# A wait on GpSimd for the VectorE instruction planned ahead of it, and output stores issued by two engines

## The chip, the cores and the metric

The program runs on one core of one Trainium2 chip. The core has five engines that each work through their own instruction list in order: TensorE (PE in the profile; PEld is its weight load), VectorE (DVE), ScalarE (ACT), GpSimd (POOL) and SyncE (SP, which here only issues DMAs). They meet through semaphores. The metric is the device time of one execution in microseconds. Before the change it is 690.68 us, the median of three runs (690.0 to 691.18). The profile was taken from one further execution of 688.92 us.

## What is computed

Three stages follow each other, all in float32 with tight precision:

```python
# 1. attention with random features, per batch and head (4 x 8 x 576 x 64, 128 features)
phi(x) = exp(h - max(h)) / sqrt(m),   h = x @ omega.T - |x|^2 / 2
num = phi(q) @ (phi(k).T @ v);  den = phi(q) @ sum_s phi(k) + 1e-6
x = num / den                            # then reshaped to 2304 tokens x 512
# 2. gated projection
x = (sigmoid(x @ w_gate) * (x @ w_val)) @ w_out        # 512 -> 1536 -> 512
# 3. soft mixture: 8 experts with 4 slots each
logits = x @ phi
slots  = softmax(logits, over tokens).T @ x             # 32 slots x 512
out    = softmax(logits, over slots) @ (max(slots @ w1[e], 0) @ w2[e])
```

## The kernel before

**Tiling.** The 2304 tokens are cut into five column blocks, four of 512 and one of 256. For stage 2 the hidden width 1536 is cut into 12 chunks of 128. A step is one block with one chunk: 12 products of 128x512 for the gate (tile `ga`), 12 for the value (tile `va`) and 12 for the way down (tiles `o0` to `o3`). There are 12 and not 4 because a float32 product is made of three passes: both operands are split into a high part in a shorter format and a low part that holds the rest, and high x high, high x low and low x high are added (function `three`). The first block is done in two pieces, with the second block between them.

**Who makes the operands.** `split_w` makes the two parts of each weight: the high part is a copy on ACT or DVE, the low part a subtraction (`w<-ws,w`, in the first steps `w<-x,w`), which POOL may do and mostly does. The three weights of a step have one tile each (`w0`, `w1`, `w2`), so POOL's subtraction for the next step has to lie between PE's last use of the tile and the first low pass that needs it. POOL also squares the attention's inputs (`g<-g`) and makes the low parts of the attention's results (`XT<-g,XT`). In the first third of the run the weights arrive as 64-bit words and are turned into float32 by a chain of integer instructions on ACT and DVE (`convert`, tile `x2T`, result in `x`), are written to DRAM (`wscr`), and are read back for the later blocks (`ws`). The attention's work is spread over the same third; its results leave PSUM through DVE and ACT (`g`, `g1b`).

**Who sets the order.** Nothing is issued as the code meets it. Every call is recorded in a `Plan` (class `Plan`, L104); `schedule` (L236) then runs a list scheduler over all of them with a cost per instruction (`cost`, L200) and writes one order for each engine, and `issue` (L398) hands the instructions out in that order. `cost` returns two values: a duration and whether the instruction holds the port that DVE and POOL share. By this table every POOL instruction holds it, and those of DVE that neither touch PSUM nor reduce. While one of the two holds it, the planner starts no port-holding instruction on the other (`port` in `schedule`). This is a rule of the plan alone. In the built program DVE and POOL wait for each other only where one reads or overwrites what the other wrote; when DVE runs later than planned, POOL starts its instruction as soon as its own inputs are there, whether or not DVE has done what was planned ahead of it.

**The end.** `combine` (L1106) makes the output in two column halves of 384 and 128 columns. PE's products go to PSUM, DVE and ACT copy them to SBUF, and `store` (L1118) issues 16 DMAs to the output, all from SP: six of 384 KB, two of 384 KB and two of 192 KB for the first half, four of 256 KB and two of 64 KB for the second.

All instructions but a few stand under one line of the profile, L405, since `issue` hands them out there; they are told apart by engine and tile.

Of the kernel before, what the change touches and what calls it, by code (L numbers as in the profile page):

```python
# [20 lines left out]
B, H, S, D, M = 4, 8, 576, 64, 128  # L21
# [7 lines left out]
HEAD, TAIL = 512, S - 512  # L29
# [74 lines left out]
class Plan:  # L104
# [95 lines left out]
    def cost(self, eng, method, kw, outs, ins):  # L200


        if method == "together":
            return TURN * (eng == "PE" and kw["parts"][0][2][0].ap[0][1] < 128) + sum(self.cost(eng, a[1], a[3], o, i)[0] for a, o, i in kw["parts"]), False
        o = outs[0] if outs else None
        n = self.free(o) if o is not None else 0
        if eng == "PE":
            if method == "transpose":
                return 0.109 * max(0.5, o.ap[0][1] / 128), False
            if ins[0].dtype == F32R:  # L210
                return (n + 32) / 2400.0, False
            if o.ap[0][1] == 32:
                return max(0.43 * n / 256, 0.055) / 4, False
            if o.ap[0][1] == 64:
                return max(n / 600.0, 0.21) / 2 + 0.12, False
            return max(0.222, n / 600.0) * (ins[0].ap[0][1] / 128 if o.ap[0][1] == 128 else 1.0), False
        ni = max([n] + [self.free(a) for a in ins])
        psum = any(a.space == bass.MemoryType.PSUM for a in ins + outs)
        if eng == "ACT":
            return (0.07 if psum else 0.11) + 0.00083 * ni + 0.09 * sum(self.free(a) == 1 for a in ins), False  # L220
        if eng == "DVE":
            if method == "reciprocal":
                return 0.06 + 0.0054 * n, False
            if method == "tensor_tensor_reduce":
                return 0.075 + ni / 960.0, False
            if method == "tensor_reduce" or psum:
                return 0.067 + ni / 960.0, False
            if method in ("tensor_tensor", "scalar_tensor_tensor"):
                return 0.067 + ni / 960.0, True
            return 0.067 + ni / 1920.0, method != "memset"  # L230
        if eng == "POOL":
            return 0.1 + 0.00225 * ni, True
        return 0.06, False
# [165 lines left out]
        assert len(order) == n, (len(order), n)  # L399
        return order  # L400

    def issue(self):
        for _, _, (e, method, a, k) in self.schedule():
            for e, method, a, k in [p[0] for p in k["parts"]] if method == "together" else [(e, method, a, k)]:
                getattr(self.eng[e], method)(*a, **k)  # L405


def body(ctx, tc, nc, qkT, tok, von, omT, wall, phi, w1, w2, ident_d, srep_d, rrep_d, mask_d, out):
    plan = Plan(nc)
    PE, ACT, DVE, POOL, SP = (Eng(plan, e) for e in ("PE", "ACT", "DVE", "POOL", "SP"))  # L410
# [6 lines left out]
    def T(shape, tag, dtype=F32, bufs=1):  # L417
        return plan.tile(sb, shape, dtype, tag, bufs)
# [12 lines left out]
    def copy(dst, src, eng=("ACT", "DVE")):  # L431
        hi_of(dst, src, eng)
# [76 lines left out]
    def turn(lst, name):  # L509
        ring[name] = ring.get(name, -1) + 1  # L510
        return lst[ring[name] % len(lst)]
# [4 lines left out]
    def bank(tag=None):  # L516
        if tag is None:
            tag = turn(FLW, "fl") if wide[0] else "fl"
        tag = "fl" if tag in POOLED else tag
        return plan.tile(psp, [128, 512], F32, tag, NFL if tag == "fl" else 1, dyn=tag == "fl")  # L520
# [585 lines left out]
    def combine(half, po):  # L1106

        (c0, w), t0 = COLS[half], plan.t
        Pf, P = (T([128, 512], "ga_a", F32, 2)[:, 0:w] for _ in range(2))
        DVE.tensor_copy(out=Pf, in_=po)  # L1110
        ps = bank("o2")[:, 0:w]
        PE.matmul(ps, rrep, Pf, start=True, stop=True)
        DVE.tensor_copy(out=P, in_=ps)
        tags = (["fl", "ga", "va", "o3", "fl", "o0"], ["fl", "ga", "va", "o3", "fl", "o0", "o1", "o2"])[half]
        rows = out.rearrange("(b s) d -> s b d", s=S)
        cols = slice(c0, c0 + w)

        def store(ob, j, z, n):  # L1118
            if j == NB - 1:
                for y in range(2):  # L1120
                    SP.dma_start(out=rows[HEAD:S, y::2, cols], in_=ob[TAIL * y:TAIL * y + TAIL])
                return
            r = S * j + 128 * z
            SP.dma_start(out=out[r:r + 128 * n, cols].rearrange("(z p) d -> p z d", p=128), in_=ob)

        def product(ps, j, z):
            r = slice(32 * z, 32 * z + 32)
            PE.matmul(ps, cT[r, j, :], P[r], start=True, stop=True)

        if half == 0:  # L1130
            tiles = [(j, z) for j in range(NB) for z in range(BLOCKS[j][1] // 128)]
            for a in range(0, len(tiles), 6):
                part6 = tiles[a:a + 6]
                plan.t = t0 + 30.0 * (a == 12)
                pb = [bank(turn(tags, "out0"))[:, 0:w] for _ in part6]
                plan.together(lambda: [product(ps, j, z) for ps, (j, z) in zip(pb, part6)])
                for k in range(0, 6, 2):
                    ob = free.pop(0)[:, 0:2 * w].rearrange("p (z d) -> p z d", z=2)
                    for y in range(2):
                        copy(ob[:, y, :], pb[k + y], (("DVE", "ACT"), ("ACT", "DVE"))[y])  # L1140
                    store(ob, *part6[k], 2)
            plan.t = t0
            return
        for js in ((0, 1), (2, 3), (4,)):
            n = BLOCKS[js[0]][1] // 128
            ob = free.pop(0).rearrange("p (j z d) -> p j z d", j=2, z=4)[:, 0:len(js), 0:n]
            pb = [bank(turn(tags, "out1"))[:, 0:w * len(js)].rearrange("p (j d) -> p j d", d=w) for _ in range(n)]
            plan.together(lambda: [product(pb[z][:, k], j, z) for k, j in enumerate(js) for z in range(n)])
            for z in range(n):
                copy(ob[:, :, z], pb[z], (("DVE", "ACT"), ("ACT", "DVE"))[z % 2])  # L1150
            for k, j in enumerate(js):
                store(ob[:, k], j, 0, n)
# [6 lines left out]
    for h in range(2):  # L1159
        r = slice(64 * h, 64 * h + 64)  # L1160
# [99 lines left out]
    i = 0  # L1260
# [50 lines left out]
        plan.t += 2.0  # L1311
        combine(half, po)
    with tc.manual_schedule():
        plan.issue()


def layout(q, k, v, omega, moe_w_gate, moe_w_val, moe_w_out, moe2_phi, moe2_w1, moe2_w2):
# [42 lines left out]
def build(nc, arrays):  # L1360
    args = [nc.dram_tensor(n, a.shape, mybir.dt.from_np(a.dtype), kind="ExternalInput").ap()
            for n, a in arrays.items()]
    args.append(nc.dram_tensor("out_0", (NTOK, DM), F32, kind="ExternalOutput").ap())
    with tile.TileContext(nc, schedule_with_timeline_sim=True) as tc:
        with ExitStack() as ctx:
            body(ctx, tc, nc, *args)
# [8 lines left out]
```

## Time and profile before

| what | value |
|---|---|
| median of three runs | 690.68 us (690.0 to 691.18) |
| the profiled execution | 688.92 us, span of its instructions 687.1 us |
| PE busy | 663.6 us, 97% |
| DVE, ACT, POOL busy | 457.7, 429.0, 288.7 us |
| TensorE's granted clock | full up to the last slice |

The span is what lies between the first and the last instruction of the profile; 1.8 us of the execution lie around it. A busy share is an average over stages that differ: PE's 97% holds a long middle in which PE hardly pauses, a start and an end where it waits for DMAs, and a few short pauses between 60 and 215 us. Idle time of another engine costs nothing unless PE waits for it there.

### The profile page before, as it was taken

The page shows a single profiled execution, that of the slowest core. Times are in us where ns is not written, and L with a number is a line of the kernel's source. Part 1 is how long each engine was busy: PE and PEld are TensorE (multiplying, and loading weights), DVE is VectorE, ACT ScalarE, POOL GpSimd, SP SyncE. Part 2 cuts the span into 40 slices and gives each one's busy share as a digit, 9 for nine tenths or more (in the row PEclk, how much of TensorE's full clock was granted, in tenths as well). Part 3 has the DMA queues.
Part 4 walks back from the last instruction along what each step waited for, and adds up shares of the span by engine and source line. Part 5 has one row for each costly group of instructions (what it writes and reads, how often), then busy time and mean ns, then how long its engine had stood idle before and what let it go on. Part 6 is the DMA issues. An engine that isn't in the chain of part 4 may idle for free.

```text
span 687.1 us, 12505 instructions
## 1 busy us (share of the span) xinstructions
PE 663.6 (97%) x4366; PEld 533.8 (78%) x4366; DVE 457.7 (67%) x1299; ACT 429.0 (62%) x962; POOL 288.7 (42%) x245
## 2 busy tenths in 40 slices
PE   7999899999999999999999999999999999999994
PEld 5676577778787888788788888788888789999672
DVE  3899999899997575666666555567444335666413
ACT  5899788888787574766566675554344445675002
POOL 0566445565334343434444543434444444553100
PEclk9999999999999999999999999999999999999997
DMA  8889766777965336443444222589622328666978
GB/s 288 314 271 326 264 208 225 264 251 245 325 239 164 114 125 217 137 133 111 136 155 152 78 62 78 159 299 321 217 93 91 101 71 292 211 203 213 404 287 275
DMA packets 50158, 139.50 MB, mean 203 GB/s; under 512 B 5552, under 2 KB 11184, under 8 KB 50096
## 3 DMA queue, kind: packets, MB, share of 16 engines
q1 hardware_dynamic: 45488, 121.94, 52.2%
q10 hardware_dynamic: 4608, 16.78, 7.2%
q8 instruction: 34, 0.56, 0.3%
q14 instruction: 28, 0.23, 0.1%
HBM read 124.54 MB, written 14.16 MB: 202 GB/s over the span
## 4 chain that ended last, share of the span: by engine, by line
PE 77%; DVE 12%; DMA 4%; ACT 2%; issue 2%; SPq 1%; POOL 0%; DVEq 0%; ACTq 0%
PE o L405 24%; PE ga L405 19%; PE va L405 19%; PE fl L405 15%; DVE x2T L405 4%; DVE g L405 3%; DVE x L405 2%; DMA wscr<-x 1%; DMA g<-in_von 1%; DVE g1b L405 1%; DMA g<-in_tok 1%; ACT ga_a L405 1%; DMA ws<-wscr 1%; DVE ga_a L405 1%; ACT g L405 1%
## 5 line engine op out<-in xcount | busy, mean ns | idle before, releaser
L405 POOL TENSOR_TENSOR w<-ws,w 128x512 fp32r<-128x512 f32 x138 | 181.4, 1315 | 253.2 <-ACT w L405 157.1
L405 PE MATMUL ga<-XT,w 128*128 128x512 f32 (+1 forms) x720 | 168.2, 376 | 1.0 <-DVE ga_a L405 0.9
L405 PE MATMUL va<-XT,w 128*128 128x512 f32 (+1 forms) x720 | 167.3, 375 | 0.4 <-DVE ga_a L405 0.4
L405 PE MATMUL o<-gt,w 128*128 128x512 f32 (+1 forms) x720 | 167.2, 376 | 0.0
L405 PEld LDWEIGHTS va<-XT,w 128*128 128x128 f32 x720 | 123.8, 189 | 26.1 <-issue 3.2
L405 PEld LDWEIGHTS ga<-XT,w 128*128 128x128 f32 x720 | 123.6, 189 | 25.9 <-DVE ga_a L405 1.8
L405 PEld LDWEIGHTS o<-gt,w 128*128 128x128 f32 x720 | 123.5, 189 | 25.3 <-issue 3.9
L405 ACT ACTIVATE w<-ws 128x512 fp32r<-128x512 f32 x107 | 67.2, 628 | 59.4 <-PE o L405 18.9
L405 PE MATMUL fl<-g,g 64*128 64x128 f32 (+4 forms) x686 | 83.8, 313 | 4.9 <-DVE g L405 2.8
L405 ACT ACTIVATE g<-g 128x128 f32<-128x128 f32 (+3 forms) x204 | 73.3, 411 | 14.1 <-DVE g L405 9.1
L405 PEld LDWEIGHTS fl<-g,g 64*128 64x128 f32 (+2 forms) x686 | 60.8, 182 | 26.6 <-DVE g L405 9.1
L405 ACT ACTIVATE ga_a<-ga_a 128x512 f32<-128x512 f32 (+1 forms) x120 | 70.0, 583 | 18.0 <-DVE ga_a L405 17.0
L405 ACT ACTIVATE ga_a<-ga 128x512 f32<-128x512 f32 (+1 forms) x60 | 33.2, 553 | 67.9 <-PE ga L405 67.8
L405 DVE SCALAR_TENSOR_TENSOR ga_a<-ga,ga_a 128x512 f32<-128x512 f32 (+1 forms) x60 | 38.0, 634 | 39.1 <-ACT ga_a L405 39.0
L405 DVE CAST w<-ws 128x512 fp32r<-128x512 f32 x55 | 23.5, 428 | 59.7 <-PE ga L405 41.1
L405 DVE TENSOR_TENSOR ga_a<-va,ga_a 128x512 f32<-128x512 f32 (+1 forms) x60 | 38.1, 634 | 18.7 <-ACT ga_a L405 13.2
L405 ACT ACTIVATE x2T<-g 128x512 f32<-128x512 f32 x72 | 45.5, 665 | 7.8 <-DVE x L405 7.8
L405 ACT ACTIVATE g1b<-g1b,g 128x128 f32<-128x128 f32 x128 | 40.4, 389 | 8.6 <-DVE g L405 8.6
L405 DVE TENSOR_SCALAR x2T<-x2T 128x512 f32<-128x512 f32 (+1 forms) x72 | 44.9, 640 | 0.7 <-ACT x2T L405 0.6
L405 DVE TENSOR_TENSOR gt<-ga_a,gt 128x512 fp32r<-128x512 f32 (+1 forms) x52 | 41.9, 805 | 2.3 <-ACT gt L405 1.3
L405 ACT ACTIVATE ga_a<-ga_a,one_b 128x512 f32<-128x512 f32 (+1 forms) x60 | 40.7, 679 | 2.7 <-issue 1.4
L405 DVE TENSOR_TENSOR g<-fl,g 64x288 f32<-64x288 f32 (+3 forms) x61 | 29.4, 483 | 17.1 <-ACT g L405 16.2
(196 smaller groups left out, 808.0 us busy)
## 6 DMA issues: line engine op xcount, KB each, us to landing
ws<-wscr SPq DMA_DIRECT2D x42, 512.0 KB, 3.6
ws<-wscr SPq DMA_DIRECT2D x78, 256.0 KB, 2.8
g<-in_wall SPq DMA_DIRECT2D x36, 512.0 KB, 4.4
g<-in_von SPq DMA_DIRECT2D x16, 640.0 KB, 6.0
wscr<-x SPq DMA_DIRECT2D x36, 256.0 KB, 3.9
g<-in_qkT SPq DMA_DIRECT2D x15, 576.0 KB, 4.9
g<-in_tok SPq DMA_DIRECT2D x15, 576.0 KB, 4.7
g<-in_w ACTq DMA_DIRECT2D x16, 512.0 KB, 6.0
```

Source lines behind the costliest of these rows:

```text
L405: getattr(self.eng[e], method)(*a, **k)
```

## The change

There are two edits. The first is in `issue`: while it hands out the instructions in the planned order, it keeps the last port-holding DVE instruction; when a port-holding POOL instruction comes, that POOL instruction is made to wait for the kept DVE instruction, which is then dropped, so that each POOL instruction waits for the last one planned ahead of it and none is waited for twice. The second is in `store`: of the first half's tail block (64 partitions, two DMAs) one DMA goes to ACT, and in the second half so do one of the two of the tail block and the stores of blocks 1 and 3. Four of the 16 stores are issued by ACT. `cost` gives such an issue 0.55 in the plan.

```diff
@@ cost
+        if eng == "ACT" and method == "dma_start" and o.tensor.name.startswith("out_"):
+            return 0.55, False
@@ issue
-    def issue(self):
-        for _, _, (e, method, a, k) in self.schedule():
+    def issue(self, tc):
+        held = {}
+        sync = mybir.DependencyInfo(mybir.DependencyClass.Sync, mybir.DependencyReason.SCHED_ONLY)
+        for _, i, (e, method, a, k) in self.schedule():
             for e, method, a, k in [p[0] for p in k["parts"]] if method == "together" else [(e, method, a, k)]:
-                getattr(self.eng[e], method)(*a, **k)
+                ins = getattr(self.eng[e], method)(*a, **k)
+            if self.cost(e, method, k, self.ops[i][4], self.ops[i][5])[1]:
+                if e == "POOL" and "DVE" in held:
+                    tc.add_manual_dep(ins.ins, held.pop("DVE").ins.name, sync, reason="port")
+                held[e] = ins
@@ combine.store
-                for y in range(2):
-                    SP.dma_start(out=rows[HEAD:S, y::2, cols], in_=ob[TAIL * y:TAIL * y + TAIL])
+                for y, q in enumerate((SP, ACT)):
+                    q.dma_start(out=rows[HEAD:S, y::2, cols], in_=ob[TAIL * y:TAIL * y + TAIL])
-            SP.dma_start(out=out[r:r + 128 * n, cols].rearrange("(z p) d -> p z d", p=128), in_=ob)
+            (SP if half == 0 or j % 2 == 0 else ACT).dma_start(out=out[r:r + 128 * n, cols].rearrange("(z p) d -> p z d", p=128), in_=ob)
```

**What it moves.** Up to the last microseconds the instructions of every engine stand in the same order as before; only the waits of POOL differ. POOL around 81 us (low parts of three weights `w`, of attention results `XT`, and a square `g`), before:

```order
L405 TENSOR_TENSOR w_170<-x_138,w_170 128x512 [waits DVE_49,Activation_49]
L405 TENSOR_TENSOR w_178<-x_138,w_178 128x512 [waits Activation_49]
L405 TENSOR_TENSOR XT<-g_80,XT 128x288 [waits Activation_49]
L405 TENSOR_TENSOR XT<-g_80,XT 128x224 [waits Activation_49]
L405 TENSOR_TENSOR XT_101<-g_80,XT_101 128x64 [waits Activation_49]
L405 TENSOR_TENSOR w_185<-x_138,w_185 128x512 [waits PE_49,Activation_49]
```

and after:

```order
L411 TENSOR_TENSOR w_170<-x_138,w_170 128x512 [waits DVE_49,Activation_49]
L411 TENSOR_TENSOR w_178<-x_138,w_178 128x512 [waits DVE_49,Activation_49]
L411 TENSOR_TENSOR XT<-g_80,XT 128x288 [waits Activation_49]
L411 TENSOR_TENSOR XT<-g_80,XT 128x224 [waits Activation_49]
L411 TENSOR_TENSOR XT_101<-g_80,XT_101 128x64 [waits DVE_49,Activation_49]
L411 TENSOR_TENSOR w_185<-x_138,w_185 128x512 [waits PE_49,DVE_49,Activation_49,Pool_49]
```

The subtraction of `w_178` now waits for DVE as well. DVE's own list at this place is the same in both kernels (ISA with `g1b` is an instruction that reads PSUM; the one behind it reads its accumulator):

```order
L405 TENSOR_REDUCE g_80<-g_78 128x10 [waits Pool_49]
L405 TENSOR_SCALAR x2T<-x2T 128x512
L405 TENSOR_SCALAR x2T<-x2T 128x512 [waits Activation_49]
L405 TENSOR_SCALAR x2T<-x2T 128x512 [waits DVE_49]
L405 ISA g1b,g_80<-fl,g_80 128x128 [waits PE_49]
L405 ISA g_80 128x1
L405 ISA g1b,g_80<-fl,g_80 128x128
L405 ISA g_80 128x1
```

The one waited for is the third TENSOR_SCALAR; the two `XT` behind it follow on POOL's queue, and `XT_101` waits for a later one. POOL between 163 and 178 us, five weights in a row (from `ws`), before:

```order
L405 TENSOR_TENSOR w_262<-ws,w_262 128x512 [waits DMAHW4_49,Activation_49]
L405 TENSOR_TENSOR w_265<-ws,w_265 128x512 [waits PE_49,DMAHW2_49,Activation_49,Pool_49]
L405 TENSOR_TENSOR w_268<-ws,w_268 128x512 [waits Activation_49]
L405 TENSOR_TENSOR w_269<-ws,w_269 128x512 [waits DMAHW3_49,Activation_49]
L405 TENSOR_TENSOR w_272<-ws,w_272 128x512 [waits DMAHW6_49,PE_49,Activation_49]
```

and after:

```order
L411 TENSOR_TENSOR w_262<-ws,w_262 128x512 [waits DMAHW4_49,DVE_49,Activation_49]
L411 TENSOR_TENSOR w_265<-ws,w_265 128x512 [waits DVE_49,PE_49,DMAHW2_49,Activation_49,Pool_49]
L411 TENSOR_TENSOR w_268<-ws,w_268 128x512 [waits DVE_49,Activation_49]
L411 TENSOR_TENSOR w_269<-ws,w_269 128x512 [waits DMAHW3_49,DVE_49,Activation_49]
L411 TENSOR_TENSOR w_272<-ws,w_272 128x512 [waits DVE_49,DMAHW6_49,PE_49,Activation_49]
```

Each of the five gains a wait for DVE; `w_262` waits for the first of three TENSOR_SCALAR `x2T` in DVE's list, behind a `gt` subtraction and one instruction of the conversion. At the very end ACT's list, before:

```order
L405 ACTIVATE XT<-o_864 128x384 [waits PE_49]
L405 ACTIVATE XT<-ga 128x2x128 [waits PE_49]
L405 ACTIVATE XT<-o_874 128x2x128 [waits PE_49]
L405 ACTIVATE XT<-ga 128x128 [waits PE_49]
L405 ACTIVATE XT<-o_872 128x2x128
L405 ACTIVATE XT<-o_876 128x2x128
```

and after:

```order
L411 ACTIVATE XT<-o_864 128x384 [waits PE_49]
L411 DMA out<-XT 64x2x384 [waits DMAHW3_49,DVE_49,Activation_49]
L411 ACTIVATE XT<-ga 128x2x128 [waits PE_49]
L411 ACTIVATE XT<-o_874 128x2x128 [waits PE_49]
L411 ACTIVATE XT<-ga 128x128 [waits PE_49]
L411 ACTIVATE XT<-o_872 128x2x128
L411 DMA out<-XT 64x2x128 [waits DMAHW5_49,DVE_49,Activation_49]
L411 DMA out<-XT 128x4x128 [waits DMAHW0_49,Activation_49]
L411 DMA out<-XT 128x4x128 [waits DMAHW2_49,DVE_49]
```

One store stands ahead of the last evictions on ACT and waits there for DVE; three stand behind them. The copy of `o_876` has gone to DVE, as its last instruction.

## Rows read from the trace of the kernel before

**Rows 1.** The page: engine, busy us, share, instructions.
```profile
PE 663.6 (97%) x4366; PEld 533.8 (78%) x4366; DVE 457.7 (67%) x1299; ACT 429.0 (62%) x962; POOL 288.7 (42%) x245
```

**Rows 2.** Busy time by stretch of the run.
```profile
core 0: us, PE busy (x) PEld busy (x) DVE busy (x) ACT busy (x) POOL busy (x), PEclk, DMA share, GB/s
60.00:110.00 50.00, 46.92 (x286) 33.61 (x284) 48.94 (x150) 42.64 (x103) 24.45 (x21) 1.00 0.75 251
...
150.00:180.00 30.00, 30.00 (x143) 25.16 (x143) 29.37 (x41) 25.81 (x49) 16.78 (x12) 1.00 0.80 269
180.00:215.00 35.00, 32.18 (x154) 25.30 (x153) 34.24 (x71) 27.74 (x56) 11.85 (x10) 1.00 0.67 231
215.00:560.00 345.00, 344.42 (x1892) 281.95 (x1891) 198.83 (x546) 198.92 (x418) 148.36 (x124) 1.00 0.44 147
```

**Rows 3.** Waits of PE and its weight load, 60 to 215 us.
```profile
PE fl L405 <- DVE g L405: 5.1, 6, 1.7
...
PEld fl L405 <- DVE g L405: 10.1, 12, 2.1
```

**Rows 4.** PE in order of time around 80 us, pauses in brackets.
```profile
79.98 1.52 PE L405 MATMUL fl<-g,g 64*128 64x128 f32 x16 [0.24 <-DVE g L405]
...
85.02 0.82 PE L405 MATMUL fl<-g,g1b 128*128 128x128 f32 x5 [1.70 <-DVE g L405]
```

**Rows 5.** DVE, then POOL, around 80 us.
```profile
76.84 1.52 DVE L405 CAST gt<-ga_a 128x512 fp32r<-128x512 f32 x1
80.94 3.19 DVE L405 TENSOR_SCALAR x2T<-x2T 128x512 f32<-128x512 f32 x3
84.05 0.28 DVE L405 CUSTOM_DVE_ANT_0 g1b<-fl,g 128x128 f32<-128x128 f32 x1
...
80.82 1.28 POOL L405 TENSOR_TENSOR w<-x,w 128x512 fp32r<-128x512 f32 x1 [2.75 <-ACT w L405]
82.06 2.25 POOL L405 TENSOR_TENSOR XT<-g,XT 128x288 fp32r<-128x288 f32 x3
```

**Rows 6.** DVE, POOL and PE in order of time, 162 to 172 us.
```profile
165.29 1.22 DVE L405 TENSOR_TENSOR gt<-ga_a,gt 128x512 fp32r<-128x512 f32 x1 [0.49 <-ACT gt L405]
166.43 0.68 DVE L405 CUSTOM_DVE_ANT_0 x<-x2T 128x1024 uint16<-128x1024 uint16 x1
167.03 2.32 DVE L405 TENSOR_SCALAR x2T<-x2T 128x512 f32<-128x512 f32 x3
171.58 0.41 DVE L405 TENSOR_SCALAR x2T<-x2T 128x512 int32<-128x512 int32 x1
...
164.22 1.74 POOL L405 TENSOR_TENSOR w<-ws,w 128x512 fp32r<-128x512 f32 x1
...
168.22 2.88 PE L405 MATMUL o<-gt,w 128*128 128x512 f32 x12
170.94 2.88 PE L405 MATMUL ga<-XT,w 128*128 128x512 f32 x12
```

**Rows 7.** DVE, POOL and PE in order of time, 202 to 210 us.
```profile
203.00 1.51 DVE L405 TENSOR_SCALAR x2T<-x2T 128x512 f32<-128x512 f32 x1
206.64 1.78 DVE L405 CUSTOM_DVE_ANT_0 x<-x2T 128x1024 uint16<-128x1024 uint16 x1
...
206.54 1.33 POOL L405 TENSOR_TENSOR w<-ws,w 128x512 fp32r<-128x512 f32 x1 [2.31 <-ACT w L405]
...
209.44 1.31 PE L405 MATMUL fl<-g,g 128*128 128x288 f32 x4 [1.65 <-DVE g L405]
```

**Rows 8.** The end: stretches (columns as in rows 2), stores on SP, an eviction.
```profile
671.00:681.00 10.00, 6.65 (x102) 4.10 (x94) 5.27 (x13) 4.07 (x11) 0.00 (x0) 0.88 1.02 348
681.00:682.00 1.00, 0.00 (x0) 0.00 (x0) 0.00 (x0) 0.00 (x0) 0.00 (x0) 0.50 0.77 221
...
L405 SPq DMA_DIRECT2D out<-XT x10: 401/638/1003, 675.2 to 682.5; - x10
...
677.11 0.38 ACT L405 ACTIVATE XT<-ga 128x256 f32<-128x256 f32 x1 [1.18 <-PE ga L405]
```

More of the change, by code (lines that the diff above doesn't have):

```diff
@@ L1313, in body @@
     with tc.manual_schedule():
-        plan.issue()
+        plan.issue(tc)
 def layout(q, k, v, omega, moe_w_gate, moe_w_val, moe_w_out, moe2_phi, moe2_w1, moe2_w2):
```

## The prediction

> **What bounds the kernel now.** I read the page's table of engines first, then busy time by stretch, then the waits of PE, and last the instructions in order of time where PE pauses. PE is busy 663.6 of 687.1 us [rows 1], and its list keeps its order, so the change can only take away pauses of PE or add some. The stretches say where they are [rows 2]: from 215 to 560 us PE is busy 344.42 of 345.00, and nothing that happens on DVE or POOL there is worth anything. From 60 to 110 us it lacks 3.1 us, from 180 to 215 us 2.8 us. In both stretches DVE is the engine that hardly stops (48.94 of 50.00, 34.24 of 35.00). From 150 to 180 us DVE is as full (29.37 of 30.00) and yet PE loses nothing: DVE's lateness costs there only when a product has to wait for it. The waits agree: between 60 and 215 us PE's attention products (`fl`) waited six times for DVE's `g`, 5.1 us in all; for the weight loads, which stand ready earlier, the same cause shows 10.1 us [rows 3]. So the most that a faster DVE can give is about 5 us, and the weight loads' 10.1 us is a bound that can't be passed.
>
> **How DVE loses time.** At 80.94 us DVE does three TENSOR_SCALAR of 128x512 and is through with them at 84.05 us, 3.1 us; one of the same size takes 0.41 us at 171.58 us [rows 5, 6]. Beside them POOL ran a subtraction of 1.28 us and three of 2.25 us in all [rows 5]. A conversion step (`x<-x2T`) takes 0.68 us at 166.43 us and 1.78 us at 206.64 us, when POOL had started 0.10 us earlier on an instruction of 1.33 us [rows 6, 7]; 1.78 is about what is left of POOL's instruction and then the step's own time. So a port-holding instruction of DVE stands still while POOL works. The change moves this: POOL now starts behind the DVE instruction that the plan has ahead of it.
>
> **A, the pauses at 80 and 85 us.** The subtraction at 80.82 us now waits for the third TENSOR_SCALAR. The three then take 3 x 0.41 = 1.2 us instead of 3.1: 1.9 us. The cast at 76.84 us took 1.52 us beside another subtraction that now also stands behind it; at 0.41 us that is 1.1 us more. DVE reaches the attention's instructions on PSUM (84.05 us) 3.0 us sooner. PE's pauses for DVE of 0.24 us at 79.98 and 1.70 us at 85.02 [rows 4] are smaller than that and go: -1.9 us. Behind DVE comes ACT, busy 42.64 of 50 us [rows 2], so no third engine is as full. What POOL does later is covered: behind the three stand instructions of DVE that read PSUM, in which POOL can run freely, and the two `XT` behind it on its queue serve a later block.
>
> **B, the pause at 209 us.** Before it DVE lost 1.1 us at 203.00 (1.51 instead of 0.41) and 1.1 us at 206.64 (1.78 instead of 0.68) to POOL instructions which now stand behind [rows 6, 7]. The 2.2 us are more than PE's pause of 1.65 us [rows 7]: -1.65 us, if nothing else is late.
>
> **The other pauses for DVE** add up to 5.1 - 0.24 - 1.70 - 1.65 = 1.5 us [rows 3, 4, 7]. They lie behind 150 us, where I expect DVE to gain little, for this reason: DVE 29.37 and POOL 16.78 of 30 us [rows 2], and between two instructions of the conversion DVE has mostly one instruction of 0.68 us in which it does not need the port, while POOL's takes 1.3. Whoever goes first, the other stands still for the rest. I leave the 1.5 us as they are. The Trainium skill says why this could hold everywhere (SBUF — State Buffer, section "Who interferes with whom"): the shared pair of ports is an exclusive lock held for a whole instruction, and "issue order, not op shape, decides who blocks". By that rule the change alone shifts who waits and A and B would have to come from DVE's instructions on PSUM behind the kept ones; that is the case at 84.05 us, and much less so from 150 to 180 us, so the sum stays.
>
> **C, POOL later, 0 to +1.2 us.** Behind a waiting POOL instruction stands all of POOL's list, and PE needs the weights. The tightest place is the subtraction at 164.22 us [rows 6]. It ended at 165.96 and the first product that reads it is the third of the twelve that begin at 168.22: at 2.72 us for twelve that is 168.22 + 2 x 0.23 = 168.68 us. It now waits for the first TENSOR_SCALAR at 167.03. Without POOL in its way DVE does the `gt` subtraction at 165.29 in 0.68 us, the conversion in 0.68 and the TENSOR_SCALAR in 0.41: 167.06 us. POOL is then through at 167.06 + 1.3 = 168.4 us, and PE loses nothing. If DVE stays as late as in the trace (167.03 + 1.52 = 168.55) POOL ends at 169.85 and PE loses 1.2 us. I take 0.3 us, near the lower end because DVE's two stretched instructions just before are gone with the cause.
>
> **D, the stores, -0.3 to +0.7 us.** The DMA engines are full from 671 to 681 us (1.02) and dip only from 681 to 682 us (0.77) [rows 8]. If the issues (0.64 us each on SP, ten in a row) are what makes the dip, issuing from two engines gives at most 0.3 us. Against it: the first store on ACT stands ahead of its last four evictions, waits for DVE and takes 0.4 to 1.0 us to issue, so the eviction at 677.11 and PE's last product behind it come about 1 us later; that is covered as long as the earlier stores still fill the DMA engines, to about 681 us, and else costs up to 0.7 us. I take -0.2. The Trainium skill (Trainium Kernel Development and Optimization, section "Key Constraints") has it that DMAs of all issuing engines run on the same 16 DMA engines and that issuing from several saves only the issue time; by it D is nothing beyond the dip, and the trace's 1.02 agrees.
>
> **The sum** is -1.9 - 1.65 + 0.3 - 0.2 = -3.45 us. The profiled execution of 688.92 us (687.1 and 1.8 around it) becomes 685.5. It lay 1.76 us under the median of the runs; carried over to the median, 690.68 - 3.45 = 687.2 us.
>
> **Rivals.** *More than that:* DVE stays ahead through 215 us, so the remaining 1.5 us go too and the weight loads' hidden part (10.1 against 5.1 us) gives another 2: 683.7 us. For it: DVE's list is full there, and each microsecond saved carries over to the next product. Against it: the port is nearly full from 150 us on. *No change:* the products at 85.02 and 209.44 us then wait for ACT, which needs PE's last result as well, or POOL's longer waits take back what DVE gains; 690.4 us. For it: ACT is busy 42.64 of 50 and 27.74 of 35 us [rows 2]. Against it: the pauses are put down to DVE alone. *Slower:* POOL's weights come too late from 150 to 180 us. PE is now without a pause there, so each delay is paid in full. If DVE stays as late as in the trace, the subtraction of 164.22 us costs 1.2 us, and with the same for the two other weights of the step 3.6 us; less A's 1.9 us that is +1.7 us, 692.4 us. It decides when POOL's instruction ends later than 168.7 us on the trace's clock. Against it: the DVE instructions that it waits for are partly late because of POOL.
>
> **Numbers.** The forecast has 0.47 (685.4 to 688.9 us on its own, by C and D's ends and A and B halved or with the hidden part), more 0.15, no change 0.20, slower 0.18. What a measurement of this kernel can tell from no change is about 0.2%, 1.4 us. Faster: nearly all of the first two, 0.62; within 0.2%: 0.20; slower 0.18. The range of 8 in 10 reaches from the rival with more to most of the way to the slower one: 683.4 to 691.7 us.
>
> **What would show it.** A: the pause in front of the `fl<-g,g1b` products near 85 us gone, and the three TENSOR_SCALAR near 81 us at 0.4 us each. B: the same near 209 us. The means of DVE's `x2T` and `gt` forms fall, DVE's busy time falls from 457.7 us by some 10, POOL's waits for DVE grow, PE's busy time stays within 1 us. C: no new wait of PE on POOL near 168 us. D: the last microseconds as full of DMA as before. It is wrong if PE's weight loads wait for POOL between 150 and 215 us, or if the pauses at 85 and 209 us stay with another engine's name.

## The result, and the profile after

The changed kernel takes 684.42 us, the median of seven runs (682.21 to 687.62), against 690.68 us (690.0 to 691.18); the ratio is 0.9915, 95% interval 0.9898 to 0.9931. The profiled execution took 683.13 us, 5.8 us less than that of before, and its span 680.9 us, 6.2 less. The forecast was 687.2 us: the direction and the two places that it counted on were right, the size too small by nearly half. 684.42 us lies under the band that the forecast had on its own (685.4 to 688.9 us) and nearest to the rival *More than that* (683.7 us), which had a chance of 0.15.

The engines of the whole run, from the page (columns as in [rows 1]):

```profile
PE 662.7 (97%) x4366; PEld 534.0 (78%) x4366; DVE 441.7 (65%) x1300; ACT 427.9 (63%) x961; POOL 284.0 (42%) x245
```

DVE is busy 16.0 us less for nearly the same work (one copy more), PE is busy 0.9 us less: nearly all that the run got shorter by was pause. The stretches of [rows 2], of the kernel after:

```profile
60.00:110.00 50.00, 49.19 (x311) 36.31 (x311) 48.35 (x154) 45.13 (x108) 24.99 (x24) 1.00 0.80 273
...
150.00:180.00 30.00, 30.00 (x154) 24.90 (x153) 27.97 (x41) 24.97 (x47) 15.33 (x11) 1.00 0.78 259
180.00:215.00 35.00, 35.00 (x179) 28.89 (x178) 33.06 (x86) 29.99 (x65) 16.12 (x14) 1.00 0.78 251
215.00:560.00 345.00, 344.43 (x1873) 281.67 (x1872) 191.93 (x529) 196.67 (x411) 147.46 (x122) 1.00 0.43 143
```

PE (first number pair after the length) has no pause left from 150 to 215 us; it lacked 2.8 us there. From 60 to 110 us 0.8 of the 3.1 us remain. Behind 215 us DVE needs 6.9 us less, and PE gains 0.01. The waits of PE from 60 to 215 us, as in [rows 3], are a single row. It isn't one of the attention's, and it stood there before at 0.7 us:

```profile
PE ga L411 <- DVE ga_a L411: 0.8, 1, 0.8
```

What became of the place at 80 us: PE, then DVE and POOL in order of time (start, length, instruction; before in [rows 4, 5]):

```profile
79.89 1.16 PE L411 MATMUL fl<-g,g 64*128 64x128 f32 x16
80.98 1.88 PE L411 MATMUL ga<-XT,w 128*128 128x512 f32 x7
82.70 1.05 PE L411 MATMUL fl<-g,g1b 128*128 128x128 f32 x8
...
80.06 1.09 DVE L411 TENSOR_SCALAR x2T<-x2T 128x512 f32<-128x512 f32 x3
81.09 0.29 DVE L411 CUSTOM_DVE_ANT_0 g1b<-fl,g 128x128 f32<-128x128 f32 x1
...
78.83 1.30 POOL L411 TENSOR_TENSOR w<-x,w 128x512 fp32r<-128x512 f32 x1 [5.53 <-DVE gt L411]
81.29 1.30 POOL L411 TENSOR_TENSOR w<-x,w 128x512 fp32r<-128x512 f32 x1 [1.16 <-DVE x2T L411]
```

No PE row has a bracket now. The three TENSOR_SCALAR take 1.09 us in all, where they took 3.19, and POOL's subtraction at 81.29 us, whose bracket says that it now waits for them, runs beside DVE's `g1b`, which read PSUM.

**Where the 6.2 us came from.** PE issues the same products in nearly the same order, so the starts of one product in the two traces can be compared. Their difference, read a few microseconds ahead of an old pause and behind it, steps there and hardly elsewhere:

| product that waited (time before) | pause before | PE gets ahead by |
|---|---|---|
| 79.98 and 85.02 us | 0.24, 1.70 | 0.67 + 1.98 |
| 104.44 us | 0.32 | 0.59 |
| 185.41, 189.25 us | 0.53, 0.64 | 0.75 + 0.85 |
| 209.44 us | 1.65 | 1.99 |
| all six | 5.08 | 6.83 |

Against these stand +0.23 us before 79 us and a new wait of PE at 629 us (+0.67); small steps and the end (-0.16) make up the rest to -6.24. Each pause gave 0.2 to 0.4 us more than its bracket. The rows show two reasons. A bracket counts from the end of the product ahead, and a product that doesn't wait starts before that end, 0.16 us in the rows above (82.70 against 80.98 + 1.88 = 82.86), 0.07 us at the first pause. And the products behind a pause take longer themselves: the four at 209.44 us took 1.31 us and take 1.13 now, the four at 185.41 us 0.66 and 0.60. At 209.44 us, with 0.15 us of the first, this makes 1.65 + 0.15 + 0.18 = 1.98 of the 1.99 us, and the other places come out within 0.02 us in the same way. (The expectations below took the steps at the waiting products themselves, which reads 0.1 to 0.2 less each.)

### The profile page after: what moved, and what is told of

It reads as the page before. It is cut to its first block, busy times and chain, and to the rows that moved or that the text cites. A ratio compares the mean times of both kernels' runs of the same rounds, so it can differ in the third digit from the quotient of the medians.

```text
span 680.9 us, 12558 instructions
## 1 busy us (share of the span) xinstructions
PE 662.7 (97%) x4366; PEld 534.0 (78%) x4366; DVE 441.7 (65%) x1300; ACT 427.9 (63%) x961; POOL 284.0 (42%) x245
## 4 chain that ended last, share of the span: by engine, by line
PE 84%; DMA 6%; DVE 3%; ACT 3%; POOL 1%; issue 1%; SPq 1%; DVEq 0%; POOLq 0%; ACTq 0%
PE o L411 24%; PE ga L411 22%; PE va L411 21%; PE fl L411 17%; DMA g<-in_tok 3%; DMA ws<-wscr 2%; DVE g L411 2%; DMA g<-in_wall 1%; ACT g L411 1%; ACT ga_a L411 1%; SPq L411 1%; POOL g L411 1%; DMA wscr<-x 1%; DVE x2T L411 1%; DVE w L411 0%
## 5 line engine op out<-in xcount | busy, mean ns | idle before, releaser
L411 DVE TENSOR_SCALAR x2T<-x2T 128x512 f32<-128x512 f32 (+1 forms) x72 | 39.7, 563 | 2.1 <-ACT x2T L411 2.1
L411 POOL TENSOR_TENSOR XT<-g,XT 128x64 fp32r<-128x64 f32 (+2 forms) x43 | 28.7, 681 | 22.9 <-ACT ga_a L411 6.7
```

Source lines behind the costliest of these rows:

```text
L411: ins = getattr(self.eng[e], method)(*a, **k)
```

## The experiments

The waits are chosen by counting POOL's instructions in the order in which they are handed out. Each kernel puts its own condition where COND stands; all but the second keep the stores of before, so that only the waits differ:

```diff
+        pool = 5
...
+                pool += e == "POOL"
...
-                    tc.add_manual_dep(ins.ins, held.pop("DVE").ins.name, sync, reason="port")
+                    kept = held.pop("DVE")
+                    if COND:
+                        tc.add_manual_dep(ins.ins, kept.ins.name, sync, reason="port")
```

Ratios are to the kernel before, run on the same chip, with 95% intervals.

**Each half alone.** All waits, stores as before; and no waits with the new stores:

```diff
-                for y, q in enumerate((SP, ACT)):
+                for y in range(2):
```

> All of GpSimd's new waits, all 16 stores on SyncE as before. Theory (the waits keep VectorE from standing still and take away TensorE's pauses before 215 us): 5.5 to 6.5 us under the kernel before, TensorE's pauses near 85, 185, 189 and 209 us gone. Rival (part of the gain comes from the stores): 4 us or less under before.

Measured: 683.25 us, 0.9894 (0.9875 to 0.9913).

```diff
-                if e == "POOL" and "DVE" in held:
-                    tc.add_manual_dep(ins.ins, held.pop("DVE").ins.name, sync, reason="port")
```

> Four stores issued by ScalarE, no new wait on GpSimd. Theory: -0.2 us, from -0.5 to +0.3; the DMA engines are full to the end. Rival (stores matter): -1.5 us or more.

Measured: 689.84 us, 0.9995 (0.9975 to 1.0014). The waits are the whole gain, the stores nothing that can be measured.

**Up to 215 us and from there.** COND is `pool < 100`, then `pool >= 100`:

> Only the waits of GpSimd's instructions planned up to about 215 us of the trace before (51 rows of its list gain or change waits); stores as before. Theory: all of the gain, 5.5 to 7 us under before, perhaps 0.6 us more than with all waits, since the pause of TensorE near 628 us is not there. Rival (the waits help everywhere by keeping VectorE free): clearly less than with all waits.

Measured: 683.36 us, 0.9895 (0.9875 to 0.9915).

> Only the waits of GpSimd's instructions planned from about 215 us on (61 rows); stores as before. Theory: no gain, 0 to +0.8 us, since TensorE is without a pause from 215 to 560 us and a wait for VectorE comes in near 628 us. Rival (help everywhere): 1.5 us or more under before.

Measured: 689.26 us, 0.9997 (0.9981 to 1.0012). That DVE gains time where PE never waits is worth nothing that can be measured, as the windows said.

**The waits at 80 us.** COND is `pool in (38, 39)`, the subtractions of `w_170` and `w_178` at 76.63 and 80.82 us of before. The text that follows counts one new wait, since the list of `w_170` has a wait for DVE in both kernels; but a list names the semaphore, not how far it has to count. The rows further down show that both waits took hold:

> One new wait alone: GpSimd's low part of w_178 (80.8 us in the trace before) waits for the third TENSOR_SCALAR planned ahead of it; stores as before. Theory (a stretched VectorE instruction just before a pause of TensorE is what the pause is made of): TensorE's pause at 85.02 us goes, 1.9 us, and nothing else changes but what hangs on it: -1.9 us, from -1.5 to -2.4. Rival (the gain needs VectorE's whole lateness to go): under 0.8 us.

Measured: 687.73 us, 0.9972 (0.9955 to 0.9989), about 1.9 us. In its trace PE gets ahead by 0.68 us at the product of 79.98 us and by 1.97 at that of 85.02, as with all waits. The first of the two subtractions, before:

```profile
76.63 1.44 POOL L405 TENSOR_TENSOR w<-x,w 128x512 fp32r<-128x512 f32 x1 [4.08 <-ACT w L405]
```

and DVE's cast and both subtractions in the kernel with these waits:

```profile
78.77 0.42 DVE L410 CAST gt<-ga_a 128x512 fp32r<-128x512 f32 x1
...
80.54 1.30 POOL L410 TENSOR_TENSOR w<-x,w 128x512 fp32r<-128x512 f32 x1 [6.06 <-DVE gt L410]
83.00 1.29 POOL L410 TENSOR_TENSOR w<-x,w 128x512 fp32r<-128x512 f32 x1 [1.16 <-DVE x2T L410]
```

The first now waits for DVE's `gt`, and the cast that took 1.52 us beside it [rows 5] takes 0.42; the second waits for the three TENSOR_SCALAR. Two semaphore waits, then, and the whole of A; what each is worth alone no run shows.

**All but 150 to 194 us.** COND is `not 73 <= pool <= 88`; all 16 stores are on SP, other than the text says:

> All of GpSimd's new waits but those of its instructions between 151 and 194 us of the trace before; stores on both engines as in the changed kernel. As the prediction argued (the shared port is full there, who goes first is no matter): the same time as the changed kernel, -6 us under before, and the pauses of TensorE near 185 and 189 us stay away. As the trace after suggests (the waits do help there): the pauses of 0.7 and 0.8 us come back, and -4.5 us under before.

Measured: 685.47 us, 0.9940 (0.9920 to 0.9961). The pauses at 185 and 189 us came back, the one at 209 us did not. So the waits behind 150 us, which I had put at nothing, were worth something. Which of them? **The first eleven** (`73 <= pool <= 83`, 151 to 176 us) **and the next five** (`84 <= pool <= 88`, 177 to 194 us), each alone:

> Only the waits of GpSimd's instructions between 151 and 176 us of the trace before, where VectorE and GpSimd together fill the shared port; stores as before. As the prediction argued (in a full port it is no matter who goes first): 0, and TensorE's pauses near 185 and 189 us as before. Theory after the waits were left out there (VectorE does instructions without the port while GpSimd has it): the pauses of 0.7 and 0.8 us shorter by 0.7 to 1.5 us together, -1 us.

Measured: 689.75 us, 1.0002 (0.9981 to 1.0024). The interval alone would not exclude a gain of 1 us; the rows below do, since the pauses are still there.

> Only the waits of the five GpSimd instructions between 177 and 194 us of the trace before; stores as before. If VectorE's time between 151 and 176 us can't be gained: the same 0.7 to 1.5 us off the pauses at 185 and 189 us comes from here alone. If it can: the pause at 185 us stays (0.7 us), the one at 189 us shrinks by VectorE's 1.1 us stretch just before it.

Measured: 686.62 us, 0.9948 (0.9929 to 0.9968): PE gets ahead by 0.73, 0.87 and 1.99 us at the three pauses, 3.6 us in all. Busy time by stretch (columns as in [rows 2]) of the kernel with the eleven waits:

```profile
150.00:177.00 27.00, 27.00 (x130) 22.54 (x129) 24.97 (x38) 24.30 (x46) 13.49 (x10) 1.00 0.76 261
177.00:195.00 18.00, 16.79 (x91) 13.21 (x90) 18.00 (x40) 13.38 (x29) 8.84 (x7) 1.00 0.83 297
```

and its products in order of time:

```profile
185.05 0.66 PE L410 MATMUL fl<-ident,g 128*128 128x128 f32 x4 [0.55 <-DVE g L410]
...
188.90 0.66 PE L410 MATMUL fl<-ident,g 128*128 128x128 f32 x4 [0.66 <-DVE g L410]
```

Busy time by stretch of the kernel with the five waits:

```profile
150.00:177.00 27.00, 27.00 (x125) 22.48 (x124) 26.38 (x40) 23.77 (x46) 15.38 (x11) 1.00 0.79 267
177.00:195.00 18.00, 18.00 (x102) 14.88 (x101) 17.79 (x47) 14.79 (x32) 5.35 (x6) 1.00 0.94 323
```

and its products:

```profile
185.34 0.60 PE L410 MATMUL fl<-ident,g 128*128 128x128 f32 x4
...
188.32 0.60 PE L410 MATMUL fl<-ident,g 128*128 128x128 f32 x4
```

The eleven waits save DVE 1.4 us of busy time up to 177 us (24.97 against 26.38), and PE still pauses behind: DVE stands idle for 2.0 of the 27 us, where it was idle for 0.6 before. 1.9 us of that are waits for ACT (three rows; the longest):

```profile
DVE x2T L410 <- ACT x2T L410: 1.2, 2, 0.7
```

A lead of 1.1 us that DVE still had against PE's products at 177 us was gone by 181 us: three subtractions of POOL, put off by the waits, ran between 175.42 and 180.29 us, and a TENSOR_SCALAR of 0.42 us took 1.52 beside them. The five waits save DVE nothing before 177 us, and the pauses go. What is different shows in DVE and POOL around 186 us of the kernel before:

```profile
186.85 1.79 DVE L405 CUSTOM_DVE_ANT_0 x<-x2T 128x1024 uint16<-128x1024 uint16 x1
...
188.91 0.28 DVE L405 CUSTOM_DVE_ANT_0 g1b<-fl,g 128x128 f32<-128x128 f32 x1
...
189.12 0.68 DVE L405 COPY g<-fl 128x512 f32<-128x512 f32 x1
...
186.80 1.30 POOL L405 TENSOR_TENSOR w<-ws,w 128x512 fp32r<-128x512 f32 x1 [3.18 <-ACT w L405]
```

and of the kernel with the five waits:

```profile
186.16 0.68 DVE L410 CUSTOM_DVE_ANT_0 x<-x2T 128x1024 uint16<-128x1024 uint16 x1
...
187.09 0.28 DVE L410 CUSTOM_DVE_ANT_0 g1b<-fl,g 128x128 f32<-128x128 f32 x1
...
187.30 0.68 DVE L410 COPY g<-fl 128x512 f32<-128x512 f32 x1
...
187.41 1.30 POOL L410 TENSOR_TENSOR w<-ws,w 128x512 fp32r<-128x512 f32 x1 [2.16 <-DMA g<-in_wall]
```

Before, POOL began 0.05 us ahead of the conversion `x`, which then took 1.79 us. Now it begins behind, 0.11 us after DVE has started to copy PSUM for 0.68 us, and neither engine stands still. `g1b`, on PSUM and close behind the kept instruction, is what PE's product at 189.25 us of before waited for (188.91 + 0.28 = 189.19).

The first of the five waits shows the other case, more port work behind the kept instruction. Before:

```profile
177.98 1.69 DVE L405 CUSTOM_DVE_ANT_0 x<-x2T 128x1024 uint16<-128x1024 uint16 x1
...
180.53 0.75 DVE L405 TENSOR_SCALAR x2T<-x2T 128x512 int32<-128x512 int32 x2
...
177.84 1.29 POOL L405 TENSOR_TENSOR w<-ws,w 128x512 fp32r<-128x512 f32 x1 [1.39 <-ACT w L405]
```

and with the five waits:

```profile
178.60 0.68 DVE L410 CUSTOM_DVE_ANT_0 x<-x2T 128x1024 uint16<-128x1024 uint16 x1
...
180.13 1.55 DVE L410 TENSOR_SCALAR x2T<-x2T 128x512 int32<-128x512 int32 x2
...
179.76 1.30 POOL L410 TENSOR_TENSOR w<-ws,w 128x512 fp32r<-128x512 f32 x1 [2.69 <-DVE x2T L410]
```

The conversion gets 1.01 us back, and the two TENSOR_SCALAR behind it lose 0.80 of that.

**Without the first and the last waits.** COND is `35 <= pool < 100`, 66 to 224 us:

> Only the waits of GpSimd's instructions between 66 and 224 us of the trace before; stores as before. Theory: the five pauses near 80, 85, 104, 185, 189 and 209 us go (6.0 us), and the 0.6 to 0.9 us that TensorE loses up to 61 us with the earlier waits do not come: -6.5 us under before, up to 0.7 us better than with all waits. Rival (VectorE must be on time from the start): no better than with all waits, -6.

Measured: 682.89 us, 0.9904 (0.9879 to 0.9929), not to be told from all waits.

**DVE waits as well.** DVE also waits for the POOL instruction planned ahead of it, so that the plan's order on the port holds both ways:

```diff
+                for x, y in (("POOL", "DVE"), ("DVE", "POOL")):
+                    if e == x and y in held:
+                        tc.add_manual_dep(ins.ins, held.pop(y).ins.name, sync, reason="port")
```

> All of GpSimd's new waits, and besides each port-holding VectorE instruction waits for the last GpSimd instruction planned ahead of it; stores as before. Theory: VectorE stands still behind GpSimd anyway when it works, but now it also waits where GpSimd is late for other reasons, and TensorE waits for VectorE: slower than with GpSimd's waits alone by 2 us or more. Rival (the plan's order of the port is right in both directions): at least 1 us faster than with GpSimd's waits alone.

Measured: 691.10 us, 1.0008 (0.9994 to 1.0022). DVE's busy time fell furthest of all, to 405.3 us, and the gain is gone. DVE's own waits for POOL in that trace (us in all, times, longest):

```profile
DVE gt L409 <- POOL w L409: 23.4, 33, 1.9
DVE x2T L409 <- POOL w L409: 15.1, 15, 1.6
```

PE waits for DVE's `g` again (4.4 us in five waits, over the run). Keeping to the planned order is not what helps; putting DVE first is.

**Other loads.** The profile after keeps about 1 us of pauses near 583 us, where PE waits for `x` from ACT and that for a reload of weights. Three of the four loads of the last expert's first weights, which lie beside it, are planned no earlier than 566 us, with all waits and then without any:

```diff
+                plan.floor = 566.0 if e == E - 1 and c else 0.0
                 ACT.dma_start(out=W1[e][c], in_=w1[e, :, 1024 * c:1024 * c + 1024])
+            plan.floor = 0.0
```

> All of GpSimd's waits, stores as before, and three of the four last loads of the experts' first weights (512 KB each, issued by ScalarE near 568 to 575 us of the trace after) are planned behind the weights that the last token block waits for; the order of the instructions behind 560 us changes with it. Theory (the pauses of 1.6 us near 583 us, and the stretch of 3.4 us at half clock that follows them in some executions, come from a 256 KB load that takes 6 to 7.4 us beside them instead of 2.6): 1 to 2.5 us faster than with the waits alone, and less spread. Rival (the pauses there are the chain of dependent steps itself): the same time within 0.7 us.

Measured: 681.81 us (680.84 to 682.88), 0.9886 (0.9864 to 0.9908).

> The kernel before, without any new wait and with its stores, and only the three late loads of the experts' first weights put behind those of the last token block. Theory (the pauses near 590 us of the trace before are that load and independent of the port): -0.7 to -1.7 us, and the executions in which half clock follows them are rarer. Rival (the gain beside the waits came from the waits' own spread): within 0.5 us of before.

Measured: 687.78 us, 0.9961 (0.9944 to 0.9977), 2.7 us (1.6 to 3.9) and more than expected. From 560 to 600 us, in the kernel after:

```profile
560.00:600.00 40.00, 38.94 (x314) 36.67 (x314) 23.25 (x56) 24.68 (x56) 20.74 (x16) 1.00 0.71 238
```

and in the one with waits and late loads:

```profile
560.00:600.00 40.00, 39.92 (x326) 37.93 (x325) 25.74 (x62) 23.98 (x55) 20.02 (x16) 1.00 0.76 252
```

The 1.0 us is there in PE's busy time, and in the last run as well (40.00 us of these 40, where before has 39.04). It has the best median of all and beats the kernel before; against the waits alone (0.9894) the intervals overlap, so that it beats those too is not shown. The surplus of 1.7 us in the last run isn't explained by these windows; by the starts of PE's products its one trace gains only 0.5 us behind 560 us.

## Why the prediction was right, and where it was short

**What bounds the kernel** held: the gain lies in PE's six pauses for DVE and nowhere else. The limit of "about 5 us" was too low by the 0.2 to 0.4 us that each pause costs beyond its bracket; the weight loads' 10.1 us was not reached either. Six pauses of 5.08 us gave 6.83. The rival with more came nearest: its first half, that the remaining pauses go too, came true. Its second, 2 us from the hidden part of the weight loads' waits, is not shown: the 1.75 us beyond the brackets are accounted for by how a bracket counts and by the longer products behind a pause.

**A** was put at -1.9 us and gave -2.65. The mechanism is as described: three TENSOR_SCALAR at 1.09 in place of 3.19 us, the cast at 0.42 in place of 1.52, POOL beside PSUM work, and two waits alone gave all of it. What was too small is the price of a pause, read from its bracket alone.

**B** was put at -1.65 and gave -1.99. Its cause was told too narrowly. The pause also goes with the five waits at 177 to 194 us alone, although POOL still runs into DVE at 202 us in that trace, and it also goes without them, when the later waits are kept: there the two instructions that B named take 0.42 and 0.68 us, as it said. Either lead is enough.

**The other pauses** are the step that failed: "They lie behind 150 us, where I expect DVE to gain little" and "I leave the 1.5 us as they are". They gave 2.19 us: 0.59 at 104 us, which doesn't even lie behind 150 us (the time should have been looked up, not inferred by subtraction), and 1.60 at 185 and 189 us. That is most of what the forecast lacked; A and B, together 1.09 us too small, and C's 0.3 us are the remainder, less the 0.9 us that PE lost elsewhere. The pause at 104 us looks like the others (the conversion ahead of it took 1.28 us at 101.45 us beside POOL, and takes 0.68), but no run tests it alone. "Whoever goes first, the other stands still for the rest" has the right number for 151 to 176 us, where the eleven waits gave 1.0002, and half of the reason: DVE's busy time did fall there, but its waits for ACT (1.9 us, where it had 0.5 before) used up a part of the lead and POOL's put-off work behind 177 us the rest. So the nothing that was forecast for this window is partly luck. And it was read from that window and carried on past it. From 177 to 194 us the row that decided was not the busy share but what stands behind the kept instruction on DVE: PSUM work, beside which POOL ran without slowing it (0.68 us for the copy at 187.30 us), and which PE awaits. The prediction had this test, "DVE's instructions on PSUM behind the kept ones", and put it to 84 us and to 150 to 180 us, not to the places of the three pauses that it left out. By the Trainium skill (SBUF — State Buffer, "Who interferes with whom") the one that issues second stands still for the whole instruction. The traces agree: 1.79 us behind a POOL start 0.05 us earlier, 0.68 without. What the order is worth has to be read from the queue behind.

**C** was put at +0.3 us and cost nothing that shows. POOL's subtraction of [rows 6] and the products that read it, after:

```profile
163.77 1.49 POOL L411 TENSOR_TENSOR w<-ws,w 128x512 fp32r<-128x512 f32 x1 [2.69 <-ACT w L411]
...
164.94 2.93 PE L411 MATMUL o<-gt,w 128*128 128x512 f32 x12
```

It ends at 165.26 us, before 164.94 + 2 x 0.23 = 165.40, when the third product needs it. PE doesn't pause; the margin is 0.14 us, so the slower rival was close here and did not come true.

**D** was put at -0.2 us, and gave -0.16 in the trace: from PE's last product to the end of the span 8.76 us instead of 9.37, with that product 0.45 us later against those ahead of it. The new stores alone show the same (8.62 us, 0.44 later). The stretches that answer to [rows 8], with the stores of before and all waits:

```profile
664.80:674.80 10.00, 6.61 (x100) 4.10 (x94) 5.27 (x13) 4.07 (x11) 0.00 (x0) 0.99 1.02 349
674.80:675.80 1.00, 0.00 (x0) 0.00 (x0) 0.00 (x0) 0.00 (x0) 0.00 (x0) 0.50 0.76 216
```

and in the kernel after:

```profile
664.80:674.80 10.00, 7.37 (x106) 4.51 (x96) 5.62 (x15) 3.72 (x10) 0.00 (x0) 0.88 1.01 344
674.80:675.80 1.00, 0.00 (x0) 0.00 (x0) 0.00 (x0) 0.00 (x0) 0.00 (x0) 0.50 0.99 263
```

The dip is filled as foreseen (0.76 to 0.99), and the later product, also foreseen, takes most of it back.

DVE's busy time fell by 16.0 us where "some 10" was said. Only the part before 215 us could matter, and of that only what stood ahead of PE's six products.

## What to carry to other kernels

When two engines share a port, ask for each collision what stands behind the instruction that goes first. If it is work that doesn't need the port and that the bounding engine awaits, making the other engine wait gave the whole stretch back here and cost nothing; if it is more work on the port, most of the gain was lost again one instruction later (0.80 of 1.01 us). Place such waits where the bounding engine pauses: here five took away three pauses and two took away two. Look up each pause in time before leaving it out. And price a pause by when its product would have started without it, not by the bracket alone.

## What the runs showed of the chip that was not expected

The same kernel's runs differ by 1 to 7 us (688.11 to 694.99 us among 21 of the kernel before), and some of it is TensorE's granted clock. In some profiles it falls to half (1.2 of 2.4 GHz) for a few microseconds behind a long pause of PE. A product near the start in the kernel after, with the pause ahead of it in brackets:

```profile
13.38 2.47 PE L411 MATMUL o<-g,g 128*128 128x128 f32 x20 [1.72 <-ACT g L411]
```

The same in the kernel with the two waits at 80 us:

```profile
13.56 1.77 PE L410 MATMUL o<-g,g 128*128 128x128 f32 x11 [3.72 <-ACT g L410]
```

and that kernel's stretch from 14 to 18 us (the third number from the end is the granted clock):

```profile
14.00:18.00 4.00, 4.00 (x24) 4.00 (x23) 0.21 (x2) 1.59 (x6) 0.00 (x0) 0.57 0.99 337
```

After the pause of 1.72 us the clock stayed full; after 3.72 us the stretch has a mean of 0.57. The length of this pause alone does not decide: the kernel with waits both ways had one of 3.01 us there and kept the full clock, the kernel with late loads alone one of 3.04 us and did not. Their stretches, in this order:

```profile
14.00:18.00 4.00, 3.48 (x32) 3.04 (x32) 0.00 (x0) 2.54 (x8) 0.26 (x1) 1.00 0.93 326
14.00:18.00 4.00, 4.00 (x25) 4.00 (x26) 0.51 (x6) 1.90 (x7) 0.00 (x0) 0.64 0.95 314
```

The clock also fell near 587 us in the kernel without the first and last waits, behind a pause for `x`:

```profile
586.11 0.33 PE L410 MATMUL fl<-ident,x2T 128*128 128x128 f32 x1 [2.18 <-ACT x L410]
```

Its stretch from 587 us, at half clock throughout:

```profile
587.00:590.00 3.00, 3.00 (x14) 3.00 (x15) 2.33 (x8) 1.33 (x4) 1.46 (x1) 0.50 0.35 93
```

In the profile of the kernel with late loads alone PE's products from 14.5 to 18.3 us lose 1.5 us against the kernel before by their starts. Whether half clock behind pauses near 583 us, in some timed runs of the kernel before, made the late loads worth 2.7 us can be asked of each run's mean clock. Among the runs with 0.994 or more the medians are 687.63 us (nine with late loads) and 689.80 us (eleven before), still 2.2 us apart: the clock is at most a small part, and the rest of the surplus stays open.
